# Values for a windowed attention: four-token rows ordered by TensorE, or 96-token rows loaded in place

## The chip, the cores and the metric

The kernel runs on one core of one Trainium2 chip. The metric is the device time of one execution in microseconds (us), as the median of several executions. The core has five engines with instruction streams of their own: PE (TensorE, matrix products; its weight loads are shown as PEld), DVE (VectorE), ACT (ScalarE), POOL (GpSimd) and SP (SyncE). Sixteen DMA engines move data between device memory (HBM) and on-chip memory (SBUF). A load that converts float32 to float16 on the way is issued by POOL and runs on queue q0. Transfers without conversion that SP issues, here the constants and the output, run on q1.

## The reference

Attention with a causal window comes first, then a soft mixture of experts over its output. There are 8 batches, 8 heads, 576 tokens and 64 values per head. Heads 0 to 3 see the last 32 tokens (plain heads), heads 4 to 7 every fourth of the last 128 (dilated heads).

```python
scores = scale * np.matmul(q, k.transpose(0, 1, 3, 2))
rel = pos[:, None] - pos[None, :]
mask_plain = (rel >= 0) & (rel < window)                                   # heads 0-3
mask_dil = (rel >= 0) & (rel < window * dilation) & (rel % dilation == 0)  # heads 4-7
attn = softmax(np.where(mask, scores, -1e9)); attn_out = attn @ v
x = attn_out.transpose(0, 2, 1, 3).reshape(4608, 512)
logits = x @ phi                                # 32 slots, 4 for each of 8 experts
slot_input = softmax(logits, axis=0).T @ x
slot_out[e] = np.maximum(slot_input[e] @ w1[e], 0.0) @ w2[e]
out = softmax(logits, axis=1) @ slot_out        # 4608 x 512, float32
```

The inputs q, k, v, w1 and w2 are float32 in device memory; the kernel computes in float16 with float32 sums.

## The kernel before

**The loop.** The work is written as one order by hand: `for b in range(B + 2): slot0(b); slot1(b); slot2(b)`, without a scheduler that moves instructions. Each engine, POOL's transfer issues included, runs its instructions in that order. `slot0(b)` (L528) makes the scores of the first plain group of batch b and the dilated outputs and transposes of batch b-1; `slot1(b)` (L562) makes the second group of scores and begins the plain outputs; `slot2(b)` (L583) makes the dilated scores, the remaining plain outputs and the logits of batch b-1. The sums over tokens for batch b-2 stand in slot 0 (`back_erow`, `back_u`).

**Loads.** All are issued by POOL. `load_qk` (L152) brings q and k of batch b+2 in slot 0, as 128 partitions with two rows of 18 tokens each (2,304 bytes as written). DVE transposes them into place (`qk_plain` L237, `qk_dil` L243), which frees the two raw buffers. `weights` (L499) issues two halves of a w1 per batch from then on, and all remaining w1 and w2 in batches 6 and 7. The compiled order on POOL lets each load wait until the load eight before it has landed.

**Values.** `load_v` (L168) brings all eight heads of v for batch b+2 in slot 1, as rows of four tokens: partition a holds tokens 4a to 4a+3 of each head, 512 bytes as written, 128 partitions and then 16 for the last 64 tokens (`sa`, `sb`). For the dilated heads this is the order the products want, up to a copy with another stride: `spread_v` (L207) copies them on DVE (L209) and twice on POOL (L212, L216). The plain heads need one token per partition. `order_v_plain` (L179) makes that order on PE, with 20 products against constant selection matrices (`orders`, L188) into the PSUM buffers of the scores, and ACT (L197) and DVE (L202) copy the result into `vP`.

**Plain tiles.** Keys and values come in five tiles of 128 tokens (the last of 64). A tile's keys meet 160 queries, 128 of its own and 32 behind them. `emit_scores` (L255) first writes the mask into PSUM with an identity product (L276), adds the score products (L287) and takes the exponent on ACT (L298). `emit_av` (L306) multiplies with the values (L344): each tile's 128 queries, and 32 more from the tile before. `emit_norm` (L353) divides on DVE, in three pieces per batch.

**End.** After the loop the slot inputs go through w1. `slot_out` (L677) multiplies with w2 and collects the slot outputs in two halves of 256 columns, the left half (0) first. The experts are taken as `ORDER` says: 0, 1, 4, 2, 3, 5, then 6 and 7, whose w2 is loaded in column halves, first both left ones, then both right ones. `combine` (L693) writes 16 output blocks in column halves, `combine_full` (L724) the other 20 in full width. SP issues the stores (L719, L743).

Of the kernel before, what the change touches and what calls it, by code (L numbers as in the profile page):

```python
# [32 lines left out]
NT = 5  # L33
TAIL = S - 4 * 128
# [4 lines left out]
WQ = 128 + WINDOW  # L39
W1 = WQ + TAIL  # L40
# [7 lines left out]
def make_masks():  # L48

    a = np.arange(128)[:, None]  # L50
    rel = np.arange(WQ)[None, :] - a
    plain = (rel >= 0) & (rel < WINDOW)
    rel = 32 + np.arange(LEFT)[None, :] - a
    left = (rel >= 0) & (rel < WINDOW) & (a < 48)
    m = [plain, plain[:, 0:TAIL]] + [left] * 5
    m = [np.where(x, 0.0, -60000.0) for x in m]
    ok = ((np.arange(128)[:, None] % 32) < LEFT) & np.ones((1, N_SLOTS), bool)
    m.append(ok)
    return np.ascontiguousarray(np.concatenate(m, axis=1).astype(np.float16))


def make_orders():

    a = np.arange(128)[:, None, None] % 32
    r = np.arange(DIL)[None, :, None]
    p = np.arange(128)[None, None, :]
    return np.ascontiguousarray((p == DIL * a + r).astype(np.float16).reshape(128, DIL * 128))
# [3 lines left out]
def kernel(  # L71
# [14 lines left out]
    orders_dram = nc.inline_tensor(make_orders(), name="orders_d")  # L86
# [5 lines left out]
    bias = (  # L92
        masks[:, None, 0:WQ].broadcast_to([128, 3, WQ]),
        masks[:, 0 : W1 + NLEFT],
        masks[:, None, 0:128].broadcast_to([128, DIL, 128]),
    )
    orders = consts.tile([128, DIL, 128], FP16, name="orders")
# [18 lines left out]
    NV = 2  # L116
    fix = tc.alloc_tile_pool(name="fix", bufs=1)
    QK_SLAB, V_SLAB = 2 * (S + 64 + S + 80 + S + S + 16), 4096
    kTp, kTd, qTp, qTd, vP, vD, vL = [], [], [], [], [], [], []
    for i in range(2):  # L120
        slab = fix.tile([128, QK_SLAB], FP16, name=f"qk{i}", tag=f"qk{i}")
        o = 0
        for dst, n in ((kTp, S + 64), (kTd, S + 80), (qTp, S), (qTd, S + 16)):
            dst.append(slab[:, o : o + 2 * n].rearrange("p (s t) -> p s t", t=2))
            o += 2 * n
    for i in range(NV):
        slab = fix.tile([128, V_SLAB], FP16, name=f"v{i}", tag=f"v{i}")
        n = NT * 4 * VW
        vP.append(slab[:, 0:n].rearrange("p (m h d) -> p m h d", m=NT, h=4))
        for dst in (vD, vL):  # L130
            dst.append(slab[:, n : n + 16 * VW].rearrange("p (h r d) -> p h r d", h=4, r=DIL))
            n += 16 * VW
# [8 lines left out]
    s_pool = tc.alloc_tile_pool(name="small", bufs=3)  # L141
    raw_pool = tc.alloc_tile_pool(name="raw", bufs=2, side="right")
# [25 lines left out]
    def load_v(b):  # L168
        slab = fix.tile([128, V_SLAB], FP16, name=f"vs_{b}", tag=f"vs{b % 2}")
        sa, sb = (slab[:, 2048 * i : 2048 * i + 2048].rearrange("a (h n) -> a h n", h=H) for i in range(2))  # L170
        vstage[b] = (sa, sb)
        nc.gpsimd.dma_start(
            out=sa, in_=v[b, :, 0:512, :].rearrange("h (a r) d -> a h (r d)", r=DIL)
        )
        nc.gpsimd.dma_start(
            out=sb[0:LEFT], in_=v[b, :, 512:S, :].rearrange("h (a r) d -> a h (r d)", r=DIL)
        )

    def order_v_plain(b):  # L179
        sa, sb = vstage[b]  # L180
        ps = [psum_s.tile([128, 2, 512], FP32, name=f"v{ab}_{b}", tag=f"s{ab}") for ab in "ab"]
        jobs = [(m, r) for r in range(DIL) for m in range(4)] + [(4, r) for r in range(DIL)]
        for m, r in jobs:
            if m < 4:
                o, l, st = ps[m // 2][:, m % 2, 0:256], orders[32 * m : 32 * m + 32, r, :], sa[32 * m : 32 * m + 32]
            else:
                o, l, st = ps[0][0:TAIL, 0, 256:512], orders[0:LEFT, r, 0:TAIL], sb[0:LEFT]
            nc.tensor.matmul(  # L188
                o.rearrange("p (h d) -> p h d", h=4),
                l,  # L190
                st[:, 0:4, D * r : D * r + D],
                start=(r == 0),
                stop=(r == DIL - 1),
                skip_group_check=True,
            )
        for ab in range(2):
            nc.scalar.copy(  # L197
                out=vP[b % NV][:, 2 * ab : 2 * ab + 2, :, 0:D],
                in_=ps[ab][:, :, 0:256].rearrange("p m (h d) -> p m h d", h=4),
            )  # L200
            if ab == 0:
                nc.vector.tensor_copy(  # L202
                    out=vP[b % NV][0:TAIL, 4, :, 0:D],
                    in_=ps[0][0:TAIL, 0, 256:512].rearrange("p (h d) -> p h d", h=4),
                )

    def spread_v(b):  # L207
        sa, sb = vstage.pop(b)
        nc.vector.tensor_copy(  # L209
            out=vD[b % NV][:, :, :, 0:D], in_=sa[:, 4:8].rearrange("a h (r d) -> a h r d", r=DIL)  # L210
        )
        nc.gpsimd.tensor_copy(  # L212
            out=vL[b % NV][32 : 32 + LEFT, :, :, 0:D],
            in_=sb[0:LEFT, 4:8].rearrange("a h (r d) -> a h r d", r=DIL),
        )
        nc.gpsimd.tensor_copy(out=vL[b % NV][0:32, :, :, 0:D], in_=vD[b % NV][96:128, :, :, 0:D])  # L216

# [19 lines left out]
    def qk_plain(ti, b):  # L237
        src = raw[(ti, b)][:, 0, :].bitcast(U32).rearrange("p (j m) -> p j m", m=32)
        t = qTp[b % 2] if ti == 0 else kTp[b % 2][:, 0:S, :]
# [15 lines left out]
    def emit_scores(b, g):  # L255
        kp, kd, qp, qd = kTp[b % 2], kTd[b % 2], qTp[b % 2], qTd[b % 2]
        jobs = []
        if g < 2:
            for m in range(3) if g == 0 else (3, 4):
                w = WQ if m < 4 else TAIL  # L260
                jobs.append((kp, 128 * m, qp, 128 * m, WQ * (m % 3), w))
            n = 3 * WQ
            if g == 1:
                for r in range(DIL):
                    w = LEFT if r < 3 else 2 * LEFT
                    jobs.append((kd, SUB * r + 96, qd, SUB * r + 128, W1 + LEFT * r, w))
                n = W1 + NLEFT
        else:
            for r in range(DIL):
                jobs.append((kd, SUB * r, qd, SUB * r, 128 * r, 128))  # L270
            n = 512
        sps = [
            psum_s.tile([128, 2, 512], FP32, name=f"s{ab}_{b}_{g}", tag=f"s{ab}") for ab in "ab"
        ]
        for h in range(4):
# [3 lines left out]
                bias[g],  # L279
# [24 lines left out]
    CHUNKS = {"p": (0, 7, 14, 20), "d": (0, 7, 14, 20)}  # L304

    def emit_av(b, kind, i):  # L306
# [3 lines left out]
        jobs, over = [], []  # L310
        for n, (t, h) in enumerate((PLAIN_UNITS if kind == "p" else DIL_UNITS)[u0:u1]):
            if kind == "p":
                g, c = divmod(t, 3)
                pt = ptile[(b, g, h // 2)]
                c0 = WQ * c
                jobs.append((0, 128, n, pt[:, h % 2, c0 : c0 + 128], vP[b % NV][:, t, h, 0 : D + 1]))
                if t > 0:
                    g, c = divmod(t - 1, 3)
                    pt = ptile[(b, g, h // 2)]
                    c0 = WQ * c + 128  # L320
                    over.append(
                        (0, 32, n, pt[:, h % 2, c0 : c0 + 32], vP[b % NV][:, t - 1, h, 0 : D + 1])
                    )
# [5 lines left out]
            else:  # L329
                pt = ptile[(b, 1, h // 2)]  # L330
                for r in range(DIL):
                    c0 = W1 + LEFT * r
# [9 lines left out]
        jobs += over  # L342
# [10 lines left out]
    def emit_norm(b, kind, i):  # L353
        u0, u1 = CHUNKS[kind][i : i + 2]
        n, o = u1 - u0, o_t.pop((b, kind, i))
        if kind == "p":
            if i == 0:
                xp_t[b] = x_pool.tile([128, NT, 4 * D], FP16, name=f"xp_{b}", tag="xp")
            x, nq = xp_t[b], 128
# [16 lines left out]
    def back_xT_plain(b, c):  # L376
# [3 lines left out]
        for t in range(NT):  # L380
            n = 128 if t < 4 else TAIL
            nc.tensor.transpose(
                rg[:, 128 * t : 128 * t + n],
                xp_t[b][0:n, t, 128 * c : 128 * c + 128],
                ident[0:n, 0:n],
# [33 lines left out]
    def back_erow(b):  # L419
        ep = ring.tile([128, NE, N_SLOTS], FP16, name=f"ep_{b}", tag="ring")  # L420
        b0 = b * S
        for t in range(NT):
            nc.tensor.transpose(
                ep[:, t, :], ET[0:32, b0 + 128 * t : b0 + 128 * t + 128], ident[0:32, 0:32]
# [17 lines left out]
    def back_u(b):  # L442
# [3 lines left out]
        for t in range(NT):  # L446
            n = 128 if t < 4 else TAIL
            for c in range(2):
                jobs.append((c, xp_t[b][0:n, t, 128 * c : 128 * c + 128], er[0:n, t, :]))
            jobs.append((4, ones[0:n, :], er[0:n, t, :]))  # L450
# [15 lines left out]
    def prologue():  # L466
# [4 lines left out]
        for i in range(2):  # L471
            nc.vector.memset(kTp[i][:, S : S + 64, :], 0.0)
            nc.vector.memset(kTd[i][:, S : S + 80, :], 0.0)
            nc.vector.memset(qTd[i][:, S : S + 16, :], 0.0)
            nc.vector.memset(vP[i][:, :, :, D : D + 1], 1.0)
            nc.vector.memset(vP[i][TAIL:128, 4, :, :], 0.0)
# [4 lines left out]
        nc.gpsimd.dma_start(out=orders.rearrange("p r n -> p (r n)"), in_=orders_dram.ap())  # L481
# [13 lines left out]
    HALVED = (6, 7)  # L495
    ORDER = (0, 1, 4, 2, 3, 5) + HALVED
    late_pools = []

    def weights(b, g):  # L499
# [3 lines left out]
        elif b == B - 2:  # L503
# [5 lines left out]
            else:  # L509
                slab_weights(4, "vs0", V_SLAB)  # L510
                load_w2(4)
        elif g == 0:
            raw_pool.release()
            pool = tc.alloc_tile_pool(name="w2b", bufs=1, side="right")
            late_pools.append(pool)
            for e in (2, 3):
                w2t[e] = pool.tile([128, 8, DMODEL], FP16, name=f"w2_{e}", tag=f"w2_{e}")
                load_w2(e)
        else:
            slab_weights(5, "vs1", V_SLAB)  # L520
            load_w2(5)
            slab_weights(6, "qk0", QK_SLAB)
            slab_weights(7, "v0", V_SLAB)
            for half in range(2):
                for e in HALVED:
                    load_w2(e, half)

    def slot0(b):  # L528
# [8 lines left out]
        if b == 0:  # L537
            nc.vector.memset(ET, 0.0)
            nc.vector.memset(siTm, 0.0)
            nc.vector.tensor_copy(out=emask[:, NE - 1, :], in_=masks[:, W1 + NLEFT :])  # L540
# [12 lines left out]
        if att and b > 0:  # L553
            order_v_plain(b)
        if b1:
# [3 lines left out]
        if b2:  # L559
            back_u(b - 2)  # L560

    def slot1(b):  # L562
# [3 lines left out]
        if att:  # L566
            emit_scores(b, 1)
            if b == 0:
                order_v_plain(b)
            spread_v(b)  # L570
# [7 lines left out]
        if b3:  # L578
            qk_plain(1, b + 1)
        if b1:  # L580
            back_xT_dil(b - 1, 1)

    def slot2(b):  # L583
# [3 lines left out]
        if att:  # L587
            emit_scores(b, 2)
            emit_av(b, "p", 1)
            emit_norm(b, "p", 1)  # L590
# [4 lines left out]
        if att:  # L595
            emit_av(b, "p", 2)
            emit_norm(b, "p", 2)
        if b3:
            qk_dil(1, b + 1, 0)
        if b1:  # L600
# [74 lines left out]
    so = [psum_so.tile([128, NH], FP32, name=f"so{i}", tag=f"so{i}") for i in range(2)]  # L675

# [120 lines left out]
```

## Time and profile before

| what | value |
|---|---|
| median of 3 runs (lowest, highest) | 184.84 us (184.61, 184.88) |
| the profiled execution, its own time | 184.61 us |
| its span, first to last instruction | 182.8 us |
| busy: PE, DVE, ACT, POOL | 142.9, 104.2, 90.1, 62.6 us |
| read from HBM, written to it | 62.18 MB, 9.44 MB |
| mean granted PE clock | 0.89 |

The span is cut into 40 equal slices, one digit or number for each. "DMA" is the mean busy share of the 16 DMA engines in tenths (9 is 90% or more), "GB/s" what they wrote. An engine's busy time is a sum over instructions; PE's are pipelined, so PE busy is not PE at its peak. For a stage, the DMA share may be above 1: an engine can have more than one packet under way, and each counts from its start to its end. A group of instructions is shown as line, engine, operation, what is written and read, and count, then busy time, the mean of one in ns, and the idle time in front of them with what ended it. A packet here is one contiguous row of a transfer, or the small one that reports its end.

### The profile page before, as it was taken

Reading aid. Unit: us, or ns where it says so; the run is one execution under the profiler, and the core shown is the slowest. Engines: PE = TensorE matmul, PEld = TensorE weight load, DVE = VectorE, ACT = ScalarE, POOL = GpSimd, SP = SyncE. Lnnn points to the kernel's source line nnn. Section 1 sums busy time; section 2 is a strip of 40 time slices with the busy share of each in tenths; the row PEclk is TensorE's granted clock in tenths of the full one; section 3 lists DMA queues with packets and bytes.
Section 4 is the critical chain, followed back from the end, with each engine's and each line's share of the span. In section 5 each row is a group of like instructions: output and inputs, shape, how many; then the busy total and the mean of one; then the engine's idle time right before and its main releaser. Section 6 shows DMA issues by size and latency. Waiting matters only on the chain.

```text
span 182.8 us, 5535 instructions
## 1 busy us (share of the span) xinstructions
PE 142.9 (78%) x2448; PEld 85.6 (47%) x2448; DVE 104.2 (57%) x225; ACT 90.1 (49%) x161; POOL 62.6 (34%) x86
## 2 busy tenths in 40 slices
PE   0467989999999999999999999998694087746600
PEld 0134556557557557557557557573532063312300
DVE  2585797958767867867867865360502004555700
ACT  2044267667666766766766766734002005644800
POOL 7643644652651751751822935311110110000000
PEclk9999999999999999999999999985569667897555
DMA  5999999999999999999999999999999999999996
GB/s 88 195 198 211 203 208 206 211 209 204 213 207 204 213 208 204 213 208 204 213 208 204 212 212 213 216 214 214 215 214 216 196 196 183 328 376 387 380 351 219
DMA packets 32024, 41.01 MB, mean 224 GB/s; under 512 B 2144, under 2 KB 19680, under 8 KB 32000
## 3 DMA queue, kind: packets, MB, share of 16 engines
q0 software_dynamic: 24640, 31.10, 97.6%
q1 hardware_dynamic: 7360, 9.56, 14.9%
q8 instruction: 19, 0.31, 0.6%
q14 instruction: 5, 0.04, 0.1%
HBM read 62.18 MB, written 9.44 MB: 392 GB/s over the span
## 4 chain that ended last, share of the span: by engine, by line
DMA 48%; PE 27%; issue 7%; ACT 6%; POOL 4%; DVE 3%; SPq 0%; POOLq 0%
DMA w<-in_moe_w_dram 34%; DMA raw<-in_q_dram 8%; DMA out_dram<-of 6%; PE lg L413 5%; PE o_p L344 5%; PE sa L287 4%; ACT p L298 4%; PE sa L276 3%; PE sb L276 3%; ACT of L732 2%; PE u L455 2%; PE rd L394 1%; PE vb L188 1%; PE va L188 1%; POOL w L220 1%
## 5 line engine op out<-in xcount | busy, mean ns | idle before, releaser
L298 ACT ACTIVATE p<-sa 128x960 f16<-128x960 f32 (+2 forms) x24 | 21.4, 890 | 30.2 <-PE sb L287 29.5
L344 PEld LDWEIGHTS <-p 128*128 128x128 f16 (+2 forms) x544 | 19.5, 98 | 12.6 <-issue 8.6
L241 DVE STREAM_TRANSPOSE qk<-raw 128x576 uint32<-128x576 uint32 x16 | 20.0, 1250 | 6.8 <-DMA raw<-in_q_dram 5.9
L250 DVE STREAM_TRANSPOSE qk<-raw 128x320 uint32<-128x320 uint32 (+1 forms) x32 | 21.5, 678 | 0.3
L298 ACT ACTIVATE p<-sb 128x960 f16<-128x960 f32 (+2 forms) x24 | 21.2, 885 | 0.0
L276 PE MATMUL sa<-masks,ident 128*128 128x480 f16 (+2 forms) x48 | 13.8, 372 | 6.6 <-DMA ident<-ident_d 4.9
L413 PE MATMUL lg<-xTd,phi 128*128 128x288 f16 x32 | 18.3, 659 | 0.0
L287 PE MATMUL sa<-qk 32*128 32x160 f16 (+4 forms) x416 | 15.7, 212 | 2.4 <-DVE qk L241 2.4
L287 PEld LDWEIGHTS <-qk 32*128 32x128 f16 x832 | 11.9, 96 | 11.8 <-issue 8.2
L276 PEld LDWEIGHTS <-ident 128*128 128x128 f16 x96 | 8.9, 102 | 17.4 <-issue 8.7
L216 POOL COPY v<-v 32x1024 f16<-32x1024 f16 x8 | 8.3, 1034 | 25.4 <-DVE v L209 22.9
L344 PE MATMUL o_p<-v,p 128*128 128x65 f16 (+1 forms) x288 | 16.4, 201 | 0.7 <-ACT v L197 0.7
L287 PE MATMUL sb<-qk 32*128 32x160 f16 (+4 forms) x416 | 15.7, 212 | 0.0
L232 POOL DMA_DIRECT2D w<-in_moe_w_dram x8 | 5.9, 742 | 27.2 <-DMA w<-in_moe_w_dram 22.8
L366 DVE TENSOR_TENSOR xp<-o_p,rc_p 128x448 f16<-128x448 f32 (+1 forms) x24 | 14.5, 602 | 0.8
L366 DVE TENSOR_TENSOR xd<-o_d,rc_d 128x448 f16<-128x448 f32 (+1 forms) x24 | 14.5, 602 | 0.8
L713 DVE TENSOR_TENSOR ot<-f,rrow 128x512 f32<-128x512 f32 x8 | 5.5, 690 | 15.8 <-PE f L697 15.6
L276 PE MATMUL sb<-masks,ident 128*128 128x480 f16 (+2 forms) x48 | 14.0, 372 | 0.4 <-issue 0.2
L681 PE MATMUL so<-w,hTm 128*32 128x256 f16 x128 | 7.0, 354 | 8.5 <-DMA w<-in_moe_w_dram 7.7
L220 POOL DMA_DIRECT2D w<-in_moe_w_dram x16 | 11.4, 715 | 5.5 <-DMA raw<-in_k_dram 2.1
L188 PE MATMUL va<-vs,orders 32*128 32x256 f16 (+1 forms) x96 | 12.1, 289 | 1.0 <-ACT p L298 1.0
L417 ACT ACTIVATE ET<-lg 128x288 f16<-128x288 f32 x16 | 6.6, 410 | 12.0 <-PE lg L413 11.8
(84 smaller groups left out, 251.7 us busy)
## 6 DMA issues: line engine op xcount, KB each, us to landing
w<-in_moe_w_dram POOLq DMA_DIRECT2D x16, 512.0 KB, 16.6
w<-in_moe_w_dram POOLq DMA_DIRECT2D x6, 1024.0 KB, 28.1
out_dram<-of SPq DMA_DIRECT2D x10, 512.0 KB, 5.5
vs<-in_v_dram POOLq DMA_DIRECT2D x8, 512.0 KB, 13.1
out_dram<-ot SPq DMA_DIRECT2D x16, 256.0 KB, 3.9
raw<-in_q_dram POOLq DMA_DIRECT2D x7, 576.0 KB, 15.1
raw<-in_k_dram POOLq DMA_DIRECT2D x7, 576.0 KB, 15.4
w<-in_moe_w_dram POOLq DMA_DIRECT2D x8, 256.0 KB, 23.3
```

Source lines behind the costliest of these rows:

```text
L188: nc.tensor.matmul(o.rearrange("p (h d) -> p h d", h=4), l, st[:, 0:4, D * r : D * r + D], start=(r == 0), stop=(r == DIL - 1), skip_group ...
L216: nc.gpsimd.tensor_copy(out=vL[b % NV][0:32, :, :, 0:D], in_=vD[b % NV][96:128, :, :, 0:D])
L220: nc.gpsimd.dma_start(out=w1t[e][:, 2 * i : 2 * i + 2, :], in_=src[:, 2 * i : 2 * i + 2, :])
L241: nc.vector.transpose(out=dst, in_=src)
L250: nc.vector.transpose(out=o, in_=i)
L276: nc.tensor.matmul(sps[h // 2][:, h % 2, 0:n], ident, bias[g], start=True, stop=False, skip_group_check=True,)
L287: nc.tensor.matmul(sps[h // 2][:, h % 2, c0 : c0 + w], kt_[32 * h : 32 * h + 32, k0 : k0 + 128, tt], qt_[32 * h : 32 * h + 32, q0 : q0 + w ...
L298: nc.scalar.activation(out=pt, in_=sps[ab][:, :, 0:n], func=AF.Exp, scale=SCALE)
L344: nc.tensor.matmul(o[p0 : p0 + np_, n, :], l, rr, start=(k == 0), stop=(k == len(jobs) - 1), skip_group_check=True,)
L366: nc.vector.tensor_tensor(out=x.rearrange("p t (h d) -> p (t h) d", h=4)[0:nq, u0:u1, :], in0=o[0:nq, 0:n, 0:D], in1=rc[0:nq, 0:n, None].b ...
L413: nc.tensor.matmul(lp, phi4[:, kc].rearrange("p c s -> p (c s)"), rhs, start=(kc == 0), stop=(kc == 3))
L681: nc.tensor.matmul(so[half][32 * a : 32 * a + 32, :], hTm[2 * g + c // 4][:, c % 4, 32 * j : 32 * j + 32], w2t[e][:, c, NH * half : NH * h ...
```

## The change

The values of the plain heads are no longer ordered on PE. They are loaded straight into `vP`, one token per partition, 96 tokens per tile at partitions 32 to 127; partitions 0 to 31 of each tile take the last 32 tokens of the tile before, by a copy on POOL. So the plain heads have six tiles of 96 queries, whose keys are 128 (32 before, 96 own), in place of five tiles of 128 keys and 160 queries. The dilated heads keep the four-token rows, with four heads per row set instead of eight. Their copy moves from DVE to ACT and one batch ahead. The value slabs become three instead of two, the staging moves to a pool of its own with two buffers, and the places where late w2 loads go change with them (expert 5 takes the place of 4 in `ORDER`). The dilated mask gets columns of its own, `orders` goes.

```diff
-NT = 5
-TAIL = S - 4 * 128
+QT = 96
+NT = S // QT
...
-WQ = 128 + WINDOW
-W1 = WQ + TAIL
+WP = NT // 2 * QT
...
-    NV = 2
+    NV = 3
...
+    vs_pool = tc.alloc_tile_pool(name="vstage", bufs=2, side="right")
...
     def load_v(b):
-        slab = fix.tile([128, V_SLAB], FP16, name=f"vs_{b}", tag=f"vs{b % 2}")
-        sa, sb = (slab[:, 2048 * i : 2048 * i + 2048].rearrange("a (h n) -> a h n", h=H) for i in range(2))
+        vt = vP[b % NV]
+        nc.gpsimd.dma_start(
+            out=vt[32:128, :, :, 0:D], in_=v[b, 0:4].rearrange("h (t a) d -> a (h t) d", t=NT)
+        )
+        sa = vs_pool.tile([128, 4, DIL * D], FP16, name=f"vsa_{b}", tag="vsa")
+        sb = vs_pool.tile([128, 4, DIL * D], FP16, name=f"vsb_{b}", tag="vsb")
         vstage[b] = (sa, sb)
         nc.gpsimd.dma_start(
-            out=sa, in_=v[b, :, 0:512, :].rearrange("h (a r) d -> a h (r d)", r=DIL)
+            out=sa, in_=v[b, 4:8, 0:512, :].rearrange("h (a r) d -> a h (r d)", r=DIL)
         )
...
-    def order_v_plain(b):
...
     def spread_v(b):
-        sa, sb = vstage.pop(b)
-        nc.vector.tensor_copy(
-            out=vD[b % NV][:, :, :, 0:D], in_=sa[:, 4:8].rearrange("a h (r d) -> a h r d", r=DIL)
-        )
+        sa, _ = vstage[b]
+        nc.scalar.copy(
+            out=vD[b % NV][:, :, :, 0:D], in_=sa.rearrange("a h (r d) -> a h r d", r=DIL)
+        )
...
+    def shift_v_plain(b):
+        vt = vP[b % NV]
+        nc.gpsimd.tensor_copy(out=vt[0:32, :, 1:NT, 0:D], in_=vt[96:128, :, 0 : NT - 1, 0:D])
...
-            for m in range(3) if g == 0 else (3, 4):
-                w = WQ if m < 4 else TAIL
-                jobs.append((kp, 128 * m, qp, 128 * m, WQ * (m % 3), w))
-            n = 3 * WQ
+            for i in range(3):
+                t = 3 * g + i
+                jobs.append((kp, QT * t, qp, QT * t, QT * i, QT))
+            n = WP
...
-    CHUNKS = {"p": (0, 7, 14, 20), "d": (0, 7, 14, 20)}
+    CHUNKS = {"p": (0, 6, 12, 18, 24), "d": (0, 7, 14, 20)}
...
     def slot0(b):
...
-        if att and b > 0:
-            order_v_plain(b)
...
+        if b3:
+            spread_v(b + 1)
...
     def slot1(b):
...
-            spread_v(b)
             if b + 2 < B:
                 load_v(b + 2)
...
+        if att:
+            emit_av(b, "p", 1)
+            emit_norm(b, "p", 1)
...
     def slot2(b):
...
             qk_dil(1, b + 1, 0)
+            spread_v_left(b + 1)
+            shift_v_plain(b + 1)
+            shift_v_left(b + 1)
...
-    ORDER = (0, 1, 4, 2, 3, 5) + HALVED
+    ORDER = (0, 1, 5, 2, 3, 4) + HALVED
```

In `weights`, w2 of expert 5 goes into the third value slab in slot 1 of batch 6; experts 2, 3 and 4 go into the space of the raw and staging buffers in slot 0 of batch 7, followed by the left half of 6; the left half of 7 and both right halves follow in slot 1.

## The prediction

> **What bounds the kernel now.** I read the page's 40 slices first, then the DMA queues and issues, then the stages, and last the instructions in order of time on ACT and POOL.
>
> ```profile
> span 182.8 us, 5535 instructions
> PE   0467989999999999999999999998694087746600
> ...
> DMA  5999999999999999999999999999999999999996
> GB/s 88 195 198 211 203 208 206 211 209 204 213 207 204 213 208 204 213 208 204 213 208 204 212 212 213 216 214 214 215 214 216 196 196 183 328 376 387 380 351 219
> ...
> q0 software_dynamic: 24640, 31.10, 97.6%
> q1 hardware_dynamic: 7360, 9.56, 14.9%
> ...
> DMA 48%; PE 27%; issue 7%; ACT 6%; POOL 4%; DVE 3%; SPq 0%; POOLq 0%
> ```
>
> The DMA row is 9 from the second slice to the last but one. PE is full too, but only until two thirds of the span; afterwards it waits. So I treat the kernel as one stream of transfers: casting loads on q0 at about 205 GB/s until 156 us, then stores at about 375 GB/s. Nothing after the loads can start earlier than they end.
>
> Is the load rate a limit or is the queue just never empty? The stages answer (columns: busy us and count of PE, PEld, DVE, ACT, POOL; granted clock; DMA share; GB/s written).
>
> ```profile
> 58.00:72.00 14.00, 13.78 (x283) 8.80 (x277) 10.80 (x23) 9.34 (x17) 6.24 (x8) 1.00 1.19 209
> 119.00:142.00 23.00, 18.13 (x277) 10.55 (x276) 6.57 (x21) 5.33 (x13) 2.96 (x4) 0.70 1.06 214
> 147.50:152.50 5.00, 2.96 (x57) 2.15 (x46) 0.00 (x0) 0.37 (x1) 0.00 (x0) 0.79 1.45 196
> ```
>
> By the packet records of the trace, 119 to 142 us moves only whole w2 rows (4,096 B as written) and 147.5 to 152.5 us only w2 halves (512 B). A 16th of 214 GB/s is 13.4 B/ns, so a 4,096 B row holds an engine for 306 ns; a 16th of 196 GB/s makes a 512 B row 41.8 ns. A straight line through both is 4.0 ns per row plus 0.0737 ns per byte. One batch in the loop is 1,152 rows of 512 B (v), 512 of 2,304 B (q, k; 174 ns by the line) and 512 of 2,048 B (w1; 155 ns): 216.6 us over 16 engines, or 13.5 us. The loop's period, from one first mask product of slot 1 to the next in the chain of waits, is 70.69 - 56.97 = 13.72 us. The loop runs within 2% of what these rows cost. Hence the end moves by whatever the change adds to the load stream, as long as loads stay queued; compute taken away buys almost nothing.
>
> **The change, part by part.**
>
> 1. *Plain half of v: added.* `load_v` now reads heads 0 to 3 as (h t) a d into 96 partitions: 96 x 24 = 2,304 rows of 64 values per batch, 256 B as read and 128 B as written, 18,432 in all. No bulk load of before has such rows. Their cost is bounded by neighbours: not under the price per byte of the best stage, 128 / 13.4 = 9.6 ns; not over a 512 B row, 41.8 ns. Between these ends I take the line, 4.0 + 9.4 = 13.5 ns. What leans to it: `phi_raw` is 512 rows of 64 B, and a fit over the packet records gives 8 to 10 ns for one, where the line says 8.7. Per engine: 18,432 / 16 x 13.5 ns = 15.55 us added (ends: 11.1 and 48.2).
>
> 2. *Same heads: removed from the old load.*
>
> ```profile
> vs<-in_v_dram POOLq DMA_DIRECT2D x8, 512.0 KB, 13.1
> ...
> vs<-in_v_dram POOLq DMA_DIRECT2D x8, 64.0 KB, 12.5
> ```
>
> 512 KB is 1,024 rows of 512 B, 64 KB 128 of them. Half go: 576 x 8 / 16 = 288 per engine at 41.8 ns, **-12.04 us**. Parts 1 and 2 together: +3.5 us (ends -0.9 and +36.1).
>
> 3. *Three transfers for v instead of two.* Eight more transfers, less one for `orders`; each ends in 16 small packets of 22 ns in the records: 7 x 22 ns = +0.15 us. `orders` (128 KB) goes and the mask table grows from 84 to 228 KB; at the read rate of the casting stage (twice 214 GB/s) these are -0.3 and +0.34 us, and they cancel.
>
> The Trainium skill weighs against this change too. "DMA: Bandwidth & Descriptors", section "Why small descriptors are slow (HBM only)", charges a 256 B descriptor 8 beats plus about 3 cycles, 11 in all; at the 850 MHz of its section "Where 436 GB/s comes from" that is 12.9 ns, and the sum of parts 1 and 2 would be an estimated +2.8 us. The same page's "Specifications" asks for at least 512 B for line rate; if that rule made a 256 B read as dear as a 512 B one (22 to 23 ns by the page's beats), the sum would be about +14 us by estimate. No bulk row of this trace decides between them.
>
> 4. *`order_v_plain` goes.* Its 160 products hold PE for about 1.2 us of a batch (54.03 to 55.19 us in the chain of waits), its two L197 copies hold ACT for 1.18, and L202 and L209 hold DVE for 0.83. Worth nothing: the loads of the same batch hide it, and the 13.5 us floor stays.
>
> ```profile
> L188 PE MATMUL va<-vs,orders 32*128 32x256 f16 (+1 forms) x96 | 12.1, 289 | 1.0 <-ACT p L298 1.0
> L216 POOL COPY v<-v 32x1024 f16<-32x1024 f16 x8 | 8.3, 1034 | 25.4 <-DVE v L209 22.9
> ```
>
> 5. *Tiles of 96 queries.* Score columns per batch fall (mask widths 480 + 304 + 512 to 288 + 368 + 512), 12 products with v go, 8 short score products, 2 transposes, 1 row transpose and 3 products for u come, and one more `emit_norm` (about 0.8 us of DVE by L365 and L366). A small gain for PE and ACT, about even for DVE; hidden as in 4.
>
> 6. *`shift_v_plain` on POOL.* 1,280 elements per partition; by L216 (1,034 ns for 1,024) 1.3 us per batch. The issue of 2,304 rows costs about 1.2 us by extension of L172 (0.88 for 1,024) and L158 (0.70 for 256). Behind both on POOL are the q and k loads. POOL is busy 6.2 of 14 us above, so it has room.
>
> 7. *A new wait on ACT.* `spread_v(b+1)` stands at the end of slot 0 of batch b and waits for values issued one batch before. Behind it on ACT is the exponent of slot 1, then PE's plain products, DVE's transposes, and through the freed raw buffers POOL's next q and k loads.
>
> ```profile
> 63.11 0.71 POOL L158 DMA_DIRECT2D raw<-in_q_dram  x1 [1.20 <-DVE qk L250]
> 65.60 0.70 POOL L158 DMA_DIRECT2D raw<-in_k_dram  x1 [1.79 <-DVE qk L250]
> ```
>
> In the compiled order each load on POOL waits for the one eight before it, so when the values land up to eight transfers are behind: w1 2.5, q and k 5.6, w1 2.5, the next values 3.3 us, in all about 14. The work from the end of slot 0 (56.97) to the k load (65.60) took 8.6 us. About 5 us of cover is left, so I cost the wait at nothing. Without the cover each of some six batches would pay the deficit.
>
> 8. *End.* w2 of experts 0, 1, 5, 2, 3, 4 whole, then the halves of 6 and 7 left, then right, as before but for the place of 4 and 5. The page's w2 bytes are unchanged, the new buffers are free long before their turn, and the last load still releases the last output: 0.
>
> Sum: 15.55 - 12.04 + 0.15 = **+3.7 us**. Against the profiled execution (184.61 us, span 182.8, 1.8 around it) 188.3; the median of the runs shown is 0.23 above it, so I say 188.5.
>
> **Rivals.**
>
> - *Small rows are dear.* A 128 B row should take 32 ns from start to end by the packet records (27 for 64 B, 60 for 512 B). Engines overlap neighbouring packets: share 1.45 in the 512 B stage. If they overlap the small ones no better, a row holds an engine 32 / 1.45 = 22 ns, and parts 1 and 2 become +13.4: **198**. For it: no bulk row under 512 B was ever run here. Against: the `phi_raw` rows. The share reached 1.9 around them, and 32 / 1.9 = 17 ns would give +7.5, which is the top of my own case.
> - *The queue runs dry.* If the wait of part 7 starts from a later landing than I think, the loads pause each batch; 1 to 2 us in six batches on top of 3.7 give **194.5 to 200.5**. The DMA row would fall below 9 in the loop.
> - *Faster.* One mechanism: in the load stream of every batch, small rows are paid by the byte. It decides from 12.04 / 1,152 = 10.45 ns per row downwards; at 9.6 the sum is -0.8: **184.0**, and with the 0.2 us by which the loop lies over its floor in each of six batches about 182.8. For it: the fitted 8 to 10 ns of still smaller rows. Against: the line has a fixed part.
> - *No difference* needs 10.0 to 10.6 ns: **184.8**, a narrow window; it is also what comes if the direct read costs as much as the ordered one.
>
> **How the numbers follow.** My case (12 to 17 ns, queue full) 0.66, with 186.6 to 192.5 as its own range; dear rows 0.17; dry queue 0.07; faster 0.06; no difference 0.04. About 0.2% is what a measurement of this kernel can tell from no change. The range leaves out the two last cases and the upper part of the dear ones: 186.4 to 196.0. Slower is 0.66 + 0.17 + 0.07 = 0.90.
>
> **What would show it.** q0 with about 38,500 packets and slightly fewer MB; loop slices near 203 GB/s with the DMA row still 9; a batch near 14.1 us; PE under 13.7 busy of 14 there and waiting for loads; the switch from about 200 to 375 GB/s some 3.7 us later and the stage after it as long as before. A row cost of 20 ns or more, or a DMA row under 9 in the loop, makes me wrong, as does a store stage whose length changes.

## The result, and the profile after

| | before | after |
|---|---|---|
| median of 4 executions (lowest, highest), us | 184.86 (184.61, 184.96) | 188.12 (187.68, 188.38) |
| the profiled execution, us (its span) | 184.61 (182.8) | 188.19 (186.3) |

The changed kernel is slower by 3.26 us; the ratio is 1.0176, with a 95% interval of 1.0154 to 1.0198. The forecast was 188.5.

The page of the changed kernel:

```profile
span 186.3 us, 5259 instructions
...
PE 127.9 (69%) x2304; PEld 78.8 (42%) x2304; DVE 103.6 (56%) x229; ACT 86.7 (47%) x153; POOL 80.2 (43%) x101
...
PE   2061048999998499999299599999788175574400
...
DMA  5999999999999999999999999999999999999996
GB/s 114 189 177 211 185 206 188 207 204 185 215 210 182 213 211 181 210 211 185 211 210 186 212 211 213 214 216 214 215 213 214 201 196 155 340 361 381 382 355 221
...
q0 software_dynamic: 38544, 30.97, 106.6%
q1 hardware_dynamic: 7360, 9.71, 14.8%
```

Compared row by row: PE's busy time is 15 us lower, and its slices now have holes (0, 2, 4, 5) where most of them had nines. The DMA row did not change: 9 throughout. The rate dips to 177 to 188 GB/s about once per batch, where the small rows pass, and is back at 204 to 215 in between. q0 moved slightly fewer megabytes in 13,904 more packets. So PE finishes its work with time to spare, and the transfers do not.

Three stages of after answer to those of before: the loop, whole w2 rows, w2 halves.

```profile
58.00:72.00 14.00, 10.83 (x182) 6.16 (x179) 7.89 (x16) 7.00 (x13) 8.43 (x10) 0.66 1.33 203
...
123.00:145.00 22.00, 18.86 (x293) 11.33 (x290) 6.74 (x21) 5.31 (x13) 3.57 (x5) 0.61 1.06 214
150.70:155.70 5.00, 3.51 (x64) 2.47 (x53) 0.00 (x0) 0.10 (x1) 0.19 (x1) 0.62 1.45 196
```

The last two have the rates of before (214 and 196). Only the loop changed, from 209 to 203 GB/s, with more packets in flight per engine (1.33 for 1.19). By the packet records a batch, from its first 128 B row to that of the next, takes 13.9 to 14.1 us in the loop; before, from 512 B row to 512 B row of the values, it was 13.55 to 13.8. PE is busy 10.83 of 14 us in this stretch, and its granted clock is down to 0.66; run 1 shows below that such a clock did not move the end.

Where the loads end and the output begins is read from the chain of waits, in order of time (start, duration, what). Before, then after:

```profile
146.53 10.42 DMA w<-in_moe_w_dram
156.99 0.32 PE so L681 x4
157.33 0.38 ACT so_sb L689
```

```profile
150.15 10.42 DMA w<-in_moe_w_dram
160.61 0.32 PE so L659 x4
160.95 0.38 ACT so_sb L667
```

The last slot output starts 3.62 us later and its wait for the last w2 is the same 10.42 us. From there to the end of the span it is 25.8 us before and 25.7 us after. The whole difference between the two spans (3.5 us) was there when the loads ended. The packet records say the same: from the first load row to the last it is 153.97 us before and 157.25 after, and the last store lands 24.69 and 24.56 us behind the last load.

### The profile page after: what moved, and what is told of

Read it like the earlier page. It is cut to its first block, busy times and chain, and to the rows that moved or that the text cites. A ratio compares the mean times of both kernels' runs of the same rounds, so it can differ in the third digit from the quotient of the medians.

```text
span 186.3 us, 5259 instructions
## 1 busy us (share of the span) xinstructions
PE 127.9 (69%) x2304; PEld 78.8 (42%) x2304; DVE 103.6 (56%) x229; ACT 86.7 (47%) x153; POOL 80.2 (43%) x101
## 3 DMA queue, kind: packets, MB, share of 16 engines
q0 software_dynamic: 38544, 30.97, 106.6%
## 4 chain that ended last, share of the span: by engine, by line
DMA 53%; PE 23%; issue 6%; ACT 6%; POOL 4%; DVE 2%; ACTq 0%; POOLq 0%; SPq 0%
DMA vsa<-in_v_dram 23%; DMA w<-in_moe_w_dram 22%; DMA out_dram<-of 5%; PE lg L384 4%; PE sa L265 4%; DMA raw<-in_q_dram 4%; PE sb L254 4%; ACT p L276 3%; PE sa L254 3%; POOL v L161 2%; PE o_p L316 2%; PE o_d L316 2%; PE f L708 1%; PE rp L353 1%; PE u L425 1%
## 5 line engine op out<-in xcount | busy, mean ns | idle before, releaser
L276 ACT ACTIVATE p<-sa 128x576 f16<-128x576 f32 (+2 forms) x24 | 19.6, 818 | 20.6 <-PE sb L265 20.4
L254 PE MATMUL sa<-masks,ident 128*128 128x288 f16 (+2 forms) x48 | 14.4, 388 | 20.1 <-ACT p L276 16.7
L177 ACT COPY v<-vsa 128x1024 f16<-128x1024 f16 x8 | 8.4, 1045 | 24.3 <-DMA vsa<-in_v_dram 24.3
L265 PE MATMUL sa<-qk 32*128 32x96 f16 (+2 forms) x448 | 16.6, 218 | 4.5 <-DVE qk L218 4.5
L276 ACT ACTIVATE p<-sb 128x576 f16<-128x576 f32 (+2 forms) x24 | 19.5, 813 | 0.0
L265 PEld LDWEIGHTS <-qk 32*128 32x128 f16 x896 | 12.9, 104 | 15.2 <-issue 10.2
L338 DVE TENSOR_TENSOR xp<-o_p,rc_p 96x384 f16<-96x384 f32 x32 | 17.7, 554 | 1.4
L265 PE MATMUL sb<-qk 32*128 32x96 f16 (+2 forms) x448 | 16.6, 219 | 0.0
L254 PE MATMUL sb<-masks,ident 128*128 128x288 f16 (+2 forms) x48 | 15.1, 406 | 0.6 <-ACT p L276 0.3
L338 DVE TENSOR_TENSOR xd<-o_d,rc_d 128x448 f16<-128x448 f32 (+1 forms) x24 | 14.5, 602 | 0.8
L358 ACT COPY xTp<-rp 128x576 f16<-128x576 f16 x16 | 10.2, 638 | 5.5 <-PE rp L353 5.5
L161 POOL DMA_DIRECT2D v<-in_v_dram x8 | 9.6, 1196 | 7.1 <-PE rd L365 3.2
## 6 DMA issues: line engine op xcount, KB each, us to landing
w<-in_moe_w_dram POOLq DMA_DIRECT2D x6, 1024.0 KB, 25.8
vsa<-in_v_dram POOLq DMA_DIRECT2D x8, 256.0 KB, 13.8
```

Source lines behind the costliest of these rows:

```text
L161: nc.gpsimd.dma_start(out=vt[32:128, :, :, 0:D], in_=v[b, 0:4].rearrange("h (t a) d -> a (h t) d", t=NT))
L177: nc.scalar.copy(out=vD[b % NV][:, :, :, 0:D], in_=sa.rearrange("a h (r d) -> a h r d", r=DIL))
L254: nc.tensor.matmul(sps[h // 2][:, h % 2, 0:n], ident, bias, start=True, stop=False, skip_group_check=True,)
L265: nc.tensor.matmul(sps[h // 2][:, h % 2, c0 : c0 + w], kt_[32 * h : 32 * h + 32, k0 : k0 + 128, tt], qt_[32 * h : 32 * h + 32, q0 : q0 + w ...
L276: nc.scalar.activation(out=pt, in_=sps[ab][:, :, 0:n], func=AF.Exp, scale=SCALE)
L338: nc.vector.tensor_tensor(out=x.rearrange("p t (h d) -> p (t h) d", h=4)[0:nq, u0:u1, :], in0=o[0:nq, 0:n, 0:D], in1=rc[0:nq, 0:n, None].b ...
```

## The experiments

My theory: the load stream sets the end, each row costs an engine a fixed part and a part per byte, and the loss is 18,432 rows at 13.4 ns for 4,608 rows at about 41.8. (A row of the new load is one token; the 96 of the title are the tokens of a tile.) Rivals: a part of the loss is the new wait on ACT, the added POOL copies or the lower PE clock; and PE's relief gives back a part, so that the rows cost more than the sum shows.

**1. The change with the old rows** (the rows undone, all else kept)

```diff
-        nc.gpsimd.dma_start(
-            out=vt[32:128, :, :, 0:D], in_=v[b, 0:4].rearrange("h (t a) d -> a (h t) d", t=NT)
-        )
-        sa = vs_pool.tile([128, 4, DIL * D], FP16, name=f"vsa_{b}", tag="vsa")
+        sa = vs_pool.tile([128, H, DIL * D], FP16, name=f"vsa_{b}", tag="vsa")
...
+        for p0, h0 in ((64, 0), (32, 4)):
+            nc.gpsimd.dma_start(
+                out=sb[p0 : p0 + LEFT],
+                in_=v[b, h0 : h0 + 4, 512:576, :].rearrange("h (a r) d -> a h (r d)", r=DIL),
+            )
...
-            nc.vector.memset(vP[i][:, :, :, D : D + 1], 1.0)
-            nc.vector.memset(vP[i][0:32, :, 0, :], 0.0)
+            nc.vector.memset(vP[i], 1.0)
```

> The changed kernel, with one thing undone: the plain heads' values are read in four-token rows of 512 B again (into the staging buffer, still three transfers per batch), and the plain products take a constant in their place, so the plain attention output is not computed from v. Everything else of the change stays: 96-query tiles, the new wait on ACT, the copies on POOL. If the loss is the rows (13.4 ns each in the profile after, 18,432 of them for 4,608 at about 41): load stream 3.3 to 3.6 us shorter, 184.6 to 184.9 us, equal to the kernel before. If the loss is the new wait, the POOL copies or the lower PE clock: it stays near 188.1. If PE work that went had any worth of its own: below 184.5.

Measured: 184.46 us beside 184.68 of before on the same chip, ratio 0.9997 (0.9978 to 1.0017). The loss is gone. The load stream is 153.70 us by the packet records, 3.55 shorter than after the change, the dips of the rate are gone, and the new wait is still there, 23 us of ACT in all:

```profile
GB/s 104 194 190 211 203 207 203 213 206 203 213 208 206 210 209 204 213 207 204 212 211 201 210 214 211 217 215 214 213 215 216 196 196 175 327 376 382 381 353 221
...
q0 software_dynamic: 24720, 30.97, 97.3%
...
L174 ACT COPY v<-vsa 128x1024 f16<-128x1024 f16 x8 | 8.4, 1046 | 23.0 <-DMA vsa<-in_v_dram 23.0
```

The mean PE clock of its profiled execution is 0.83, below that of after (0.85). So the wait, the copies, the clock and the third transfer are not the loss. The median lies 0.1 us under what was expected and just under 184.5, the sign for a worth of PE's relief; but the interval takes in no change, so nothing of such a worth can be measured.

**2. Before without the ordering of the values** (the relief alone)

```diff
     def order_v_plain(b):
+        return
```

> The kernel before, with the ordering of the plain values left out (no selection products on PE, no copies out of PSUM; the plain products take a constant, so the plain attention output is not computed from v). Loads are the same. If loads bound it: 184.5 to 184.9 us, no change, with PE idle about 1.2 us more per batch. If PE bounds the loop: 1.2 us for each of some seven batches, near 177.

Measured: 184.54 beside 184.68, ratio 0.9989 (0.9975 to 1.0004). PE, ACT and DVE lose 5.6, 7.1 and 1.3 us of busy time, and the end stays. Its loop stage has the rate of before to the digit:

```profile
58.00:72.00 14.00, 13.90 (x268) 8.69 (x266) 11.43 (x25) 9.78 (x17) 6.25 (x8) 1.00 1.19 209
```

PE was expected to idle 1.2 us more per batch; it is shown busy for 13.90 of 14 us here although work was taken away. The drawn length of a product is not its work: the logits product of 128 x 288 is drawn with 658 ns where it reads `xTd` and with 291 where it reads `xTp`. What fills the row here was not worked out, but a full PE row was no sign of a PE limit.

**3. Before with the new rows** (the rows alone)

```diff
...
         nc.gpsimd.dma_start(
-            out=sa, in_=v[b, :, 0:512, :].rearrange("h (a r) d -> a h (r d)", r=DIL)
+            out=direct[32:128, :, 0:D], in_=v[b, 0:4].rearrange("h (t a) d -> a (h t) d", t=6)
         )
         nc.gpsimd.dma_start(
-            out=sb[0:LEFT], in_=v[b, :, 512:S, :].rearrange("h (a r) d -> a h (r d)", r=DIL)
+            out=sa, in_=v[b, 4:8, 0:512, :].rearrange("h (a r) d -> a h (r d)", r=DIL)
+        )
+        nc.gpsimd.dma_start(
+            out=sb[0:LEFT], in_=v[b, 4:8, 512:S, :].rearrange("h (a r) d -> a h (r d)", r=DIL)
...
     def order_v_plain(b):
-        sa, sb = vstage[b]
+        sa, sb = fixed, fixed
```

> The kernel before with all of its compute and its order, but the plain heads' values loaded in rows of 128 B as in the change (three transfers per batch); the selection products read a constant in their place, so the plain attention output is not computed from v. If the rows are the whole loss: +3.3 to +3.7 us, 188.2 to 188.6. If the new order, the wait on ACT or the POOL copies make a part of the loss: less than that by their part. If a PE that is as full as before cannot keep the slower stream fed: more.

Measured: 187.86 beside 184.68, ratio 1.0175 (1.0155 to 1.0195): +3.2 us, the loss of the whole change, with PE nearly as full as before.

```profile
58.00:72.00 14.00, 13.35 (x270) 8.31 (x267) 10.37 (x22) 9.03 (x17) 7.30 (x9) 1.00 1.32 203
```

The loop is at 203 GB/s with a share of 1.32, as after the change (203 and 1.33), though here the granted clock is 1.00 and PE has all of its old work. Runs 1 to 3 together leave the new way of reading the plain values as the one cause. Their size and the places where they land changed together; the price of a 128 B row, below, is enough for the whole loss.

**4. The change with the wait later**

```diff
-        if b3:
-            spread_v(b + 1)
...
             qk_dil(1, b + 1, 0)
+            spread_v(b + 1)
             spread_v_left(b + 1)
```

> The changed kernel, with the ACT copy of the next batch's dilated values moved from the end of slot 0 to the end of slot 2, so that ACT no longer stands 24 us in all before it while values land. If the wait is covered by loads under way, as the prediction says: 188.1, no change (within 0.3 us). If part of the loss is this wait: lower by up to 1 to 3 us.

Measured: 187.84 beside 184.68, ratio 1.0167 (1.0148 to 1.0186), which overlaps that of the change (1.0154 to 1.0198). ACT's stand before this copy fell from 24.3 to 15.1 us:

```profile
L177 ACT COPY v<-vsa 128x1024 f16<-128x1024 f16 x8 | 8.4, 1046 | 15.1 <-DMA vsa<-in_v_dram 15.1
```

Nine microseconds less of waiting moved the end by at most a few tenths. The wait is covered by loads that are under way.

**5. Still smaller rows**

```diff
-        nc.gpsimd.dma_start(
-            out=vt[32:128, :, :, 0:D], in_=v[b, 0:4].rearrange("h (t a) d -> a (h t) d", t=NT)
-        )
+        src = v[b, 0:4].rearrange("h (t a) d -> a (h t) d", t=NT)
+        for c in range(0, D, D // 2):
+            nc.gpsimd.dma_start(out=vt[32:128, :, :, c : c + D // 2], in_=src[:, :, c : c + D // 2])
```

> The changed kernel with the plain heads' values loaded in two transfers of half the columns each: 36,864 rows of 64 B in place of 18,432 of 128 B, and one transfer more per batch. If a row costs 4.0 ns and 0.0737 ns per byte, a 64 B row is 8.7 ns: 2,304 x 8.7 = 20.0 us per engine for 15.4, and 8 transfers more 0.2 us: +4.8, 192.9 us. If rows are paid by the byte: 188.3. If each row below some size costs the same (13.4 ns): +15.6, 203.7 us. The eight-transfer limit of POOL is tighter here, so a dry queue would show as DMA slices below 9 in the loop and would come on top.

Measured: 195.48 beside 184.81, ratio 1.0586 (1.0557 to 1.0615), 7.4 us above the change where the line asked for 4.8. The direction is the theory's, the size is not. In the profiled execution, the slowest of the six (196.60), the load stream is 165.76 us by the packet records, 8.51 more than after the change.

Is the price of a 64 B row what was wrong? The trace has 1.15 us (10.47 to 11.63 us) in which only such rows are under way, and 2,206 of them start in it: 16 x 1,151 / 2,206 = 8.3 ns each on one of 16 engines, where the line said 8.7. In the same way 1,159 rows of 128 B in 0.94 us after the change make 13.0 ns. The batches agree: from the first 64 B row of one to that of the next it is 14.5 to 14.6 us in the loop (15.6 once), 0.4 to 0.7 more than after the change, and the line asked for 0.6. So the line holds for single rows down to 64 B, and some 4 of the 8.51 us are not the price of rows.

About 2.2 of them stand at the very end. From the moment when fewer than 16 load packets are under way to the last load row it is 3.4 us before, 3.9 after and 6.0 here: with fewer packets than engines some engines have no load left, and the last slot output waits for the last row. Why they end further apart here was not tried, nor where the rest went. POOL now stands longer ahead of its w1 loads until earlier loads have landed, as the expectation feared (total, times, longest in us); after the change, then here:

```profile
POOL w L197 <- DMA w<-in_moe_w_dram: 1.8, 1, 1.8
```

```profile
POOL w L197 <- DMA w<-in_moe_w_dram: 10.9, 9, 1.8
```

```profile
DMA  5999999999999999999999999999999999899996
GB/s 104 188 145 210 149 206 154 192 210 158 199 211 168 197 212 172 192 210 175 196 211 175 191 211 212 217 213 213 215 216 214 201 193 133 268 367 380 382 354 207
```

The DMA row stays at 9 through the loop; the one 8 stands where the loads hand over to the stores. With several packets under way per engine (a share of 1.41 over 4 to 180 us) a 9 does not show that every engine had work at every moment.

**6. One expert halved instead of two**

```diff
-    HALVED = (6, 7)
-    ORDER = (0, 1, 4, 2, 3, 5) + HALVED
+    HALVED = (7,)
+    ORDER = (0, 1, 4, 2, 3, 5, 6) + HALVED
...
```

The whole w2 of expert 6 is then loaded ahead of the two halves of 7, and `slot_out` takes it with the first seven experts.

> The kernel before with only expert 7's w2 in column halves, expert 6's whole: 2,048 rows of 512 B become 256 of 4,096 B, 128 x 41.8 - 16 x 306 ns = 0.45 us off the load stream. If rows are all that counts: 184.3 to 184.4 us. Against it: the left half of 7 now lands only about 2.7 us before the right one, not 5.4, so the first stores may come too late to fill the queue; then 185 to 187.

Measured: 187.38 beside 184.81, ratio 1.0132 (1.0113 to 1.0151). Fewer rows, and slower: the second branch of the expectation, a little above its range. The loads are 0.2 us shorter (153.77 for 153.97; 0.45 was expected), but the first store now starts 1.48 us after the last load; before, it started 1.93 us ahead of it.

```profile
DMA  5999999999999999999999999999999993999996
GB/s 90 200 198 212 202 207 208 212 205 207 213 204 208 212 205 210 210 204 210 212 204 209 212 212 218 210 217 216 214 213 214 209 178 47 334 368 377 380 351 216
```

One slice falls to 3 and 47 GB/s. I read this so: the small rows of the second halved expert buy the time in which the first output is made; another order of the halves was not tried. Fewer rows helped only as long as the queue stayed full.

**7 to 9. Wider stores**

```diff
-            out=out[r0 : r0 + 256, :].rearrange("(k p) n -> p k n", k=2), in_=ot
+            out=out[r0 : r0 + 256, :].rearrange("(p k) n -> p k n", k=2), in_=ot
...
+    def rows_of(blk):
+        if blk < NSPLIT:
+            return ET[:, 128 * blk : 128 * blk + 128]
+        r0 = 256 * (blk // 2)
+        return ET[:, r0 : r0 + 256].rearrange("s (p k) -> s k p", k=2)[:, blk % 2, :]
```

The products for the output and for the row sums take `rows_of(blk)` as weights. Run 7 puts this on run 6, run 8 on the kernel before, run 9 on the changed kernel.

> As the run with one halved w2, and the 20 full output blocks are stored two neighbouring token rows per partition: 1,280 rows of 4,096 B in place of 2,560 of 2,048 B. The output packets of the records (46 ns for 1,024 B, 86 for 2,048) leave about 6 ns that a row costs whatever its size: 80 rows fewer per engine, 0.4 to 0.5 us off the store stage, if that stage is bound by its rows. Then 0.4 to 0.5 below the run with one halved w2. If the stage is bound by bytes or by memory: no difference from that run. The products read their weights with a stride of two here.

> The kernel before, with nothing changed but the 20 full output blocks stored two neighbouring token rows per partition (1,280 rows of 4,096 B for 2,560 of 2,048 B). The run with one halved w2 became about 0.56 us faster by this (187.38 to 186.82). If the store stage is bound by its rows: 0.4 to 0.6 below before, 184.2 to 184.4 us, faster than both kernels. If the gain there came only from filling the gap ahead of the stores: no difference, 184.8.

> The changed kernel with the same wide stores. If the load stream and the store stage are one sum: the same 0.4 to 0.6 off, 187.5 to 187.7 us, and the distance to the kernel before with wide stores stays at 3.3. If the two hide each other: another distance.

| run | us | beside before | ratio (95% interval) |
|---|---|---|---|
| 7, on run 6 | 186.82 | 184.81 | 1.0098 (1.0081 to 1.0116) |
| 8, on before | 183.61 | 184.54 | 0.9938 (0.9918 to 0.9957) |
| 9, on after | 187.21 | 184.54 | 1.0140 (1.0118 to 1.0162) |

Run 8 is faster than both kernels, by 0.9 us of before and about 4.5 of after. By the medians the gain is 0.56 on run 6 and 0.93 on before; on after it is 0.59, each kernel taken beside the before of its own set (2.67 us above it with the wide stores, 3.26 without). The sum of rows asked for 0.4 to 0.6, and runs 8 and 9 both came out below the times expected. The distance between runs 9 and 8 is 3.6 us, between after and before 3.3; with intervals of some 0.4 to 0.6 us the two are not told apart, so load stream and store stage add up. The same 12 us of the store stage, before and in run 9:

```profile
164.00:176.00 12.00, 5.93 (x22) 2.80 (x21) 6.28 (x9) 6.45 (x13) 0.00 (x0) 0.61 1.03 378
```

```profile
164.00:176.00 12.00, 7.63 (x27) 3.21 (x25) 6.74 (x11) 6.58 (x14) 0.00 (x0) 0.72 1.02 407
```

The window of before ends with 1 us of 1,024 B rows. From 165 to 175 us, where nearly all rows are those of full blocks in both, the same view gives 381 and 406 GB/s at shares of 1.03 and 1.02. The 5.24 MB of the full blocks take 13.8 us at the one rate and 12.9 at the other, which is about the gain of run 8.

## Why the prediction was right

- *The bound.* Right, but for one sentence: stores can start before the loads end. The first store of before starts 1.93 us ahead of the last load, and run 6 shows that this is worth time. The stream of loads sets the end: runs 1 and 2 change the load of PE, ACT and DVE by several microseconds without moving it, run 3 moves it with their work unchanged.
- *Parts 1 and 2, the rows.* Right, size included. The line said 13.5 ns for a 128 B row. A fit over the packet records of after (rows of each size that start in a short stretch, against the time of 16 engines) gives 13.4, other ways of fitting them 12 to 13.7, and the stretch in which only such rows are under way 13.0. From start to end such a row took 32 ns, as said. The line was drawn through 512 and 4,096 B and carried on to 128; that it holds there, and for single rows of 64 B too (8.3 ns in run 5, where it said 8.7), makes this more than a lucky number. The Trainium skill's 11 cycles ("DMA: Bandwidth & Descriptors", "Why small descriptors are slow (HBM only)") come to an estimated 12.9 ns at the page's 850 MHz, close below. The same page's 512 B for line rate ("Specifications") is no step in price here: the rate within a row of 256 B read falls to 19 B/ns from 24.5 for one of 1,024 B.
- *Part 3, one more transfer, the constants.* Not told apart. Run 1 has the third transfer and the larger mask table too and shows no loss.
- *Parts 4 and 5, the work taken away.* Right: nothing that runs 1 and 2 can measure.
- *Part 6, POOL.* Right: 1,196 ns for the issue of 2,304 rows (said: 1.2 us), POOL busy 8.4 to 9.9 of 14 us in the loop. Between 18 and 150 us the records never have fewer than 14 load packets under way, before and after alike, so no pause in the loads came of it.
- *Part 7, the wait.* Right in its price. It is longer than I would have guessed, up to 9.3 us at once and 24.3 in all, in which ACT stands until the values land:

```profile
L177 ACT COPY v<-vsa 128x1024 f16<-128x1024 f16 x8 | 8.4, 1045 | 24.3 <-DMA vsa<-in_v_dram 24.3
```

- *Part 8, the end.* Right: 25.8 and 25.7 us.
- *The sum.* +3.7 said; +3.26 between the medians, +3.58 between the profiled executions, +3.28 for the load stream. With 13.4 ns in place of 13.5 it would have been 3.55, with 13.0 it would have been 3.09. What is left is within the scatter of the runs.
- *The rivals.* Dear rows (22 ns) fell with the fit. A dry queue is ruled out by the 14 packets of part 6 and by the batch of 13.9 to 14.1 us, which is what its rows cost by the line (14.0); the DMA row alone could not, as with a share of 1.33 a 9 can hide a pause. Rows paid by the byte would have made after equal or faster; run 5 shows a price per row as well.
- *The signs.* q0's packets (38,544), the loop's 203 GB/s, a batch of 13.9 to 14.1 us and a store stage of the old length came as said. PE under 13.7 busy of 14 did not come everywhere: two windows of the loop after, 44 to 58 and 72 to 86 us, have 13.77 and 13.85.

## What to carry to other kernels

Where the DMA row is full and stages without compute run at the rate of the busy ones, price the transfers first: take the rate of stages with one row size each, draw the line through them, and count rows. Work taken off a full PE bought nothing there, and the arrangement on chip that let the loads keep long rows was free. A row saved counted only while the queue stayed full; slower rows that bridge the hand-over from loads to stores can be worth more than they cost (run 6). The line prices rows, not all of the stream: with very many small rows the engines also ended further apart (run 5).

## What the runs showed that was not expected

- Run 5 lost 8.51 us of load stream where the rows account for about half. Alone, a 64 B row held an engine for 8.3 ns, as the line says; 2.2 us more went by at the end of the loads, when fewer than 16 load packets were under way (6.0 us, 3.9 after the change).
- In run 2, PE was shown as busy for 13.90 of 14 us after work was taken from it; busy time of a pipelined engine did not tell a limit.
- Stores of 4,096 B rows ran at 406 GB/s where 2,048 B rows ran at 381 (run 9 and before, 165 to 175 us).
